# Rows and logits of an attention and mixture-of-experts kernel from one set of products on split rows, with expert weights laid out by the host

## The chip, the cores and the metric

The kernel runs on one core of one Trainium2 chip. The metric is the device time of one execution in microseconds, as the median of several runs; lower is better. The core has five engines that each work through an instruction stream of their own, in order: TensorE (PE, matrix products), VectorE (DVE), ScalarE (ACT), GpSimd (POOL) and SyncE (SP, which here issues almost all DMA transfers). Weight loads of PE are shown apart as PEld.

## The reference, cut to what matters

```python
def _attn_ref(u, v, z):                    # u, v: 8 x 2496 x 256, z: 8 x 2496 x 64
    scores = (1.0 / S) * np.matmul(z, z.transpose(0, 2, 1))
    attn = np.maximum(scores, 0.0) ** 2
    return u * np.matmul(attn, v)

def _moe_ref(x, modality_id, w_gate, modality_bias, w1, w2):   # x: 19968 x 256, 8 experts
    logits = x @ w_gate + modality_bias[modality_id]
    e_idx = np.argmax(logits, axis=1)
    gate_w = softmax(logits)[np.arange(N), e_idx]
    for e in range(E):
        mask = e_idx == e
        h = np.maximum(x[mask] @ w1[e], 0.0)                   # 256 -> 1024
        out[mask] = gate_w[mask, None] * (h @ w2[e])           # 1024 -> 256
```

The output of the attention, one row of 256 for each of 19968 tokens, is the input of the mixture of experts. Each token goes to the one expert with the largest logit.

## The kernel before, in words

**Precision.** Most products run in a rounded 32-bit type (`F32R`) that TensorE takes in one pass. To keep precision, an operand is split into a high part, its rounded copy, made by ACT or DVE, and a low part, the difference, made by DVE; then three products (high x high, high x low, low x high) replace one. What is handed to TensorE as plain 32-bit floats shows two recorded passes for each product.

**Attention stage.** There are 8 batches. The 2496 queries of a batch are cut into five chunks (`NCH`) of 512 columns, the last of 448. A chunk goes through ten steps (`NI`), each over 256 keys. A step forms the scores (`scores`, L307), takes ReLU and the square on ACT (`root`, `square`), splits the squares (`high`, `low`) and multiplies them with the split v (`weigh`, L418), adding up in PSUM. The 128 rows of the contraction are used as two halves of 64 that run side by side, so each accumulator exists twice; the two are added on the way out. Scores are symmetric: the squares of one block are turned by DVE in 32 x 32 blocks (`turn_squares`, L332), stored to HBM (`store_squares`, four to six DMA issues), and loaded later for the mirrored block (`load_turned`), which saves its scores.

**The end of a chunk.** The result lies with the 256 features on partitions (two groups of 128) and tokens along the free dimension, in the column order that the host has given to z and u. `evacuate_low` (ACT, L465) copies one accumulator half, `evacuate_high` (DVE, L469) adds the other, `weigh_u` (DVE, L476) multiplies with u. Then `make_gates` (PE, L492) forms the 8 logits of each token: for each of four tiles of 128 tokens and two groups of features a product in plain 32-bit floats on each half of the rows, 128 token columns stationary and the 8 gate columns moving. `take_gates` copies one half (ACT, L503) and adds the other (DVE, L505). `make_rows` (PE, L529) turns the same columns into rows by 16 transpositions against an identity matrix, and `take_rows` (ACT, L538, twice) puts them into the tile `x` of 128 tokens x 4 x 258, whose last two columns later take gate weight and token number. After a batch's last chunk the routing (`route_logits` to `route_slots`, mostly DVE, two small counting products on PE at L610) finds each token's expert and its place there, and GpSimd scatters the rows into the experts' lists `xs` in HBM by indirect DMA (`scatter`, L646), 20 for a batch.

**Expert weights.** `lay_weights` copies the weights from HBM to HBM into the layout that the expert stage loads: w1 of an expert in two copies (L206), its rows regrouped in blocks of 32, w2 in one copy (L211). These 24 copies are issued during batches two to seven, three to a batch's worth of steps.

**The order of the work.** The instruction order of every engine in the attention stage is written out by a planner when the program is built: each piece of work has an engine, a price in us, a due time in steps (`need`), predecessors with a lag, and buffers that it takes and gives back (`room`: 6 PSUM banks, 6 `zm` buffers, 7 `x` tiles and so on; 8 `lane`s stand for outstanding transfers of SP's queue). The planner keeps a clock for each engine and gives it the most urgent piece that is ready. On the chip every engine then follows that fixed order and waits by semaphore. The last chunk of the last batch is finished inside the expert stage (`between`).

**Expert stage.** From about 1390 us on: tiles of 512 tokens of one expert, up (L1224), ReLU and split (L1228, L1229), down (L1237, L1238), the weighted sum (L1272, L1275), and an indirect DMA that puts rows in place (L1247). The change touches only its first tile and the routing that lies in it.

Of the kernel before, what the change touches and what calls it, by code (L numbers as in the profile page):

```python
# [9 lines left out]
F32 = mybir.dt.float32  # L10
F32R = mybir.dt.float32r
# [4 lines left out]
P = 128  # L16
# [10 lines left out]
def tile_attention_moe(ctx: ExitStack, tc: tile.TileContext, ut, v, zt, mid, wg, mb, w1, w2, out):  # L27
# [15 lines left out]
    E, _, F = w1.shape  # L43
# [50 lines left out]
    def bank_tile(shape, name):  # L94
        return bank["pool"].tile(shape, F32, tag=bank["tag"], name=name)
# [73 lines left out]
    gate = small.tile([P, KD, E], F32, name="gate_w")  # L169
    small_raw = {}  # L170

    def load_gate():
        nc.sync.dma_start(out=gate, in_=wg.rearrange("(k p) e -> p k e", p=P))

# [27 lines left out]
    def lay_weights(e, n):  # L202
        if n == 0:

            for k in range(KD):
                nc.sync.dma_start(  # L206
                    out=w1s[e, :, k, :].rearrange("(b q) f -> b q f", q=BLK),
                    in_=w1[e].rearrange("(b k q) f -> k b q f", k=KD, q=BLK)[k],
                )
        else:  # L210
            nc.sync.dma_start(out=w2s[e], in_=w2[e].rearrange("(j p) d -> p j d", p=P))  # L211
# [47 lines left out]
    def load_u(b, c):  # L259
        x = rows.tile([P, KD, T], F32, tag="u", bufs=1, name="ut")  # L260
        nc.sync.dma_start(out=x, in_=ut[b, :, :, c * T:(c + 1) * T].rearrange("k p q -> p k q"))
        U[b, c] = x
# [192 lines left out]

    def evacuate_low(b, c, h):

        w = width[c]
        if not h:
            x = rows.tile([P, J, XW], F32, tag="x", bufs=NCH + 2, name="x")  # L460
            t = x.rearrange("p j c -> p (j c)")[:, 0:KD * T].rearrange("p (k t) -> p k t", k=KD)
            if w < T:
                nc.gpsimd.memset(t[:, :, w:T], 0.0)
            oT[b, c] = (t, x)
        nc.scalar.copy(out=oT[b, c][0][:, h, :w], in_=acc[b, c][1][h][:, :w])  # L465

    def evacuate_high(b, c, h):
        y = oT[b, c][0][:, h, :width[c]]
        nc.vector.tensor_tensor(out=y, in0=acc[b, c][0][h][:, :width[c]], in1=y, op=ALU.add)  # L469
        if not h:  # L470
            acc.pop((b, c))

    def weigh_u(b, c):

        t = oT[b, c][0]
        nc.vector.tensor_tensor(out=t, in0=t, in1=U.pop((b, c)), op=ALU.mult)  # L476

    turned_rows, gates = {}, {}

    def make_gates(b, c):  # L480

        t = oT[b, c][0]
        if b == B - 1 and c == NCH - 1:
            parts = [bank_tile([P, J, E], "pg")]
            rows_of = (slice(0, P),)
        else:
            parts = [bank_tile([P, J, E], "pg") for _ in halves]
            rows_of = halves
        for j in range(J):
            for dh in range(KD):  # L490
                for x, h in zip(parts, rows_of):
                    nc.tensor.matmul(  # L492
                        out=x[:, j, :], lhsT=key_columns(t[h, dh], c * J + j), rhs=gate[h, dh, :],
                        start=dh == 0, stop=dh == KD - 1,
                    )
        gates[b, c] = parts

    def take_gates(b, c, n):
        if c == 0 and n == 0:
            LG[b] = rows.tile([P, NCOL, E], F32, tag="lg", bufs=2, name="lg")  # L500
        y = LG[b][:, c * J:(c + 1) * J, :]
        if n == 0:
            nc.scalar.copy(out=y, in_=gates[b, c][0])  # L503
        else:
            nc.vector.tensor_tensor(out=y, in0=gates[b, c][1], in1=y, op=ALU.add)  # L505

    def make_last_rows(b, c):

        t, x = oT[b, c]
        parts = [bank_tile([P, J // 2, D], "po") for _ in range(2)]  # L510
        for j in range(J):
            for dh in range(KD):
                nc.tensor.transpose(  # L513
                    out=parts[j // 2][:, j % 2, dh * P:(dh + 1) * P], in_=key_columns(t[:, dh], c * J + j), identity=ident
                )
        turned_rows[b, c] = (parts, x)

    def take_last_rows(b, c, n):
        parts, x = turned_rows[b, c]
        nc.scalar.copy(out=x[:, n * J // 2:(n + 1) * J // 2, 0:D], in_=parts[n])  # L520
        X[b, c] = x

    def make_rows(b, c):
        t, x = oT[b, c]
        parts = [bank_tile([P, J, KD, DK], "po") for _ in halves]
        for j in range(J):
            for dh in range(KD):
                for r, h in enumerate(halves):
                    nc.tensor.transpose(  # L529
                        out=parts[r][:, j, dh, :], in_=key_columns(t[h, dh], c * J + j), identity=ident[h, h]  # L530
                    )
        turned_rows[b, c] = (parts, x)

    def take_rows(b, c, r):

        parts, x = turned_rows[b, c]
        y = x[:, :, 0:D].rearrange("p j (k h d) -> p j k h d", k=KD, h=2)[:, :, :, r, :]
        nc.scalar.copy(out=y, in_=parts[r])  # L538
        if r:
            del turned_rows[b, c]  # L540
            X[b, c] = x
# [351 lines left out]
    def transfer(us, need, f, *args, issues=1, take=(), **more):  # L893
        p = piece("Q", us, need, f, *args, take=[*take, *(Hold("lane") for _ in range(issues))], **more)
        p.issues = issues
        return p

    def piece(on, us, need, f, *args, after=(), take=(), drop=(), gate=-1):
# [6 lines left out]
        "zr": 3, "vr": 3, "x": NCH + 2, "u": 1, "lane": 8,  # L905
    }
    LEAD = 3.6
    MADE = 2
# [18 lines left out]
    def z_pieces(b, c):  # L927
        need = uses_z[b, c][0] - LEAD
        read = None
        if b:  # L930
            hold_zr[b, c] = Hold("zr")
            read = transfer(0.7, need - 4, load_z, b, c, take=[hold_zr[b, c]], gate=need - 25)
        high = piece("A", 0.55, need - 1, prep_z_high, b, c, after=[read], take=[hold_z[b, c]])
        done_z[b, c] = piece("D", 0.65, need - 0.6, prep_z_low, b, c, after=[high], drop=[hold_zr[b, c]])
        begun.append(done_z[b, c])
# [74 lines left out]
    def chunk_pieces(b, c):  # L1010
# [24 lines left out]
        taken[b, c] = [g1] + took  # L1035
        whole = c == NCH - 1 and b < B - 1
        if whole or b == B - 1 and c == 1:
            route_pieces(b, WHOLE if whole else SOON, end + 1.5, [p for k in range(c + 1) for p in taken[b, k]])
# [23 lines left out]
    transfer(0.3, 2, load_gate)  # L1062
# [7 lines left out]
    for e in range(E):  # L1070
        for k in range(2):
            n = 2 * e + k
            transfer(3.2, (1 + n // 3) * per + NI + NI // 2 * (n % 3), lay_weights, e, k, issues=1 if k else 2, gate=(1 + n // 3) * per + NI - 2 + NI // 2 * (n % 3))
# [25 lines left out]
    with tc.manual_schedule(engines={ET.PE, ET.Activation, ET.DVE, ET.Pool, ET.SP}):  # L1099
# [25 lines left out]
        releases, moved = [], 0.0  # L1125
# [26 lines left out]
        while left:  # L1152
# [24 lines left out]
            if e == "Q":  # L1177
                clock[e] = now + 0.4 * p.issues
                moved = max(clock[e] + 0.5, moved) + p.us
                p.end = moved + 1.1  # L1180
                releases += [(p.end, "lane")] * p.issues
# [19 lines left out]
        weigh_u(B - 1, NCH - 1)  # L1201
# [167 lines left out]
    between[0][1] += [lambda: make_last_rows(B - 1, NCH - 1)]  # L1369
    between[0][1] += [lambda: make_gates(B - 1, NCH - 1), lambda: take_gates(B - 1, NCH - 1, 0)]  # L1370
    between[0][2] += [lambda: take_last_rows(B - 1, NCH - 1, 0), lambda: take_last_rows(B - 1, NCH - 1, 1)]
# [8 lines left out]
    for slot, pieces in ((3, (route_logits, route_exp)), (4, (route_places,)), (5, (route_gates,)), (6, (route_count,)), (7, (route_slots,))):  # L1380
        put(slot, *(lambda p=p: p(B - 1, LATE) for p in pieces))
    for n, k in enumerate(range(LATE.start, NCOL)):
        put(8 + n * 5 // 6, lambda k=k: scatter(B - 1, k))
    planning = plan()
    for slot in (9, 10, 11, 12, 13):
        put(slot, lambda: next(planning, None))
# [84 lines left out]
```

## Time and profile before

| | |
|---|---|
| median of 3 runs | 2282.15 us (2278.42 to 2285.0) |
| profiled execution | 2283.72 us, span of its instructions 2281.9 us |
| mean granted clock of TensorE | 0.984 |
| busy: PE, DVE, ACT, POOL | 2235.4, 1555.8, 1338.1, 351.7 us |
| gate products, L492 | 1264 records, 85.2 us busy |
| transposes of rows, L529 | 624 records, 41.7 us busy |
| HBM read and written | 246.49 MB, 140.96 MB |

All figures below the first row come from one profiled execution. In rows of groups, "busy" is the time in which at least one instruction of the group ran and the mean is the duration of one; products overlap (weight load, two halves of the rows, pipeline), so a mean is not the time that a product takes from its successor. In a timeline row the first number is the start, the second how long the row's instructions lasted together, and `x32` how many of them are merged; a bracket gives the idle time before it and what ended it.

### The profile page before, as it was taken

The page shows a single profiled execution, that of the slowest core. Times are in us where ns is not written, and L with a number is a line of the kernel's source. Part 1 is how long each engine was busy: PE and PEld are TensorE (multiplying, and loading weights), DVE is VectorE, ACT ScalarE, POOL GpSimd, SP SyncE. Part 2 cuts the span into 40 slices and gives each one's busy share as a digit, 9 for nine tenths or more (in the row PEclk, how much of TensorE's full clock was granted, in tenths as well). Part 3 has the DMA queues.
Part 4 walks back from the last instruction along what each step waited for, and adds up shares of the span by engine and source line. Part 5 has one row for each costly group of instructions (what it writes and reads, how often), then busy time and mean ns, then how long its engine had stood idle before and what let it go on. Part 6 is the DMA issues. An engine that isn't in the chain of part 4 may idle for free. (4 is left out here: it accounts for less than half of the span.)

```text
span 2281.9 us, 43759 instructions
## 1 busy us (share of the span) xinstructions
PE 2235.4 (98%) x17166; PEld 1941.6 (85%) x17166; DVE 1555.8 (68%) x2163; ACT 1338.1 (59%) x1695; POOL 351.7 (15%) x342
## 2 busy tenths in 40 slices
PE   9999999999899999999999999999999999999997
PEld 8888988788799789799888888888888888888886
DVE  8667667677577767667877766666666666666664
ACT  8647658557457557557657663455555555554553
POOL 0000300300300300300300311211121212112121
PEclk9999999999999999999999999999999999999999
DMA  7975875884784884794884972554454545455450
GB/s 165 242 208 119 227 223 112 226 230 90 214 234 101 229 230 110 197 251 109 210 228 106 206 195 53 143 155 139 139 155 123 167 120 157 125 153 144 134 160 23
DMA packets 601378, 373.66 MB, mean 164 GB/s; under 512 B 487594, under 2 KB 550570, under 8 KB 596426
## 3 DMA queue, kind: packets, MB, share of 16 engines
q1 hardware_dynamic: 586074, 329.57, 56.6%
q0 software_dynamic: 15088, 41.21, 4.8%
q8 instruction: 136, 2.23, 0.4%
q14 instruction: 80, 0.66, 0.1%
HBM read 246.49 MB, written 140.96 MB: 170 GB/s over the span
## 5 line engine op out<-in xcount | busy, mean ns | idle before, releaser
L394 DVE TENSOR_TENSOR al<-r,ah 128x1024 fp32r<-128x1024 f32 (+1 forms) x359 | 422.3, 1191 | 85.4 <-ACT ah L385 77.0
L418 PE MATMUL acc<-ah,vh 64*128 64x512 f32 (+1 forms) x3120 | 465.9, 391 | 5.4 <-ACT x L465 3.1
L1237 PE MATMUL po<-w,hh 128*128 128x512 f32 x1248 | 449.9, 397 | 0.0
L418 PE MATMUL acc<-ah,vl 64*128 64x512 f32 (+1 forms) x3120 | 449.8, 385 | 0.0
L418 PE MATMUL acc<-al,vh 64*128 64x512 f32 (+1 forms) x3120 | 449.4, 384 | 0.0
L1224 PE MATMUL ph<-xh,w 128*128 128x512 f32 x1248 | 426.3, 392 | 0.5 <-ACT lg L503 0.3
L1228 ACT ACTIVATE hh<-ph 128x512 fp32r<-128x512 f32 x312 | 186.5, 598 | 381.7 <-PE ph L1224 381.5
L1229 DVE SCALAR_TENSOR_TENSOR hl<-ph,hh 128x512 fp32r<-128x512 f32 x312 | 215.8, 692 | 231.1 <-ACT hh L1228 231.1
L646 POOL DMA_INDIRECT xs<-x,sloti x160 | 193.9, 1212 | 1159.0 <-ACT r L315 516.2
L418 PEld LDWEIGHTS acc<-ah,vh 64*128 64x128 f32 x3120 | 327.8, 188 | 50.7 <-ACT x L465 6.0
L315 ACT ACTIVATE r<-s 128x1024 f32<-128x1024 f32 (+2 forms) x244 | 247.0, 1013 | 199.1 <-PE s L307 180.3
L418 PEld LDWEIGHTS acc<-al,vh 64*128 64x128 f32 x3120 | 328.5, 186 | 41.0 <-DVE al L397 0.8
L418 PEld LDWEIGHTS acc<-ah,vl 64*128 64x128 f32 x3120 | 323.9, 187 | 41.9
L1238 PE MATMUL po<-w,hl 128*128 128x256 f32 x1248 | 350.2, 281 | 0.0
L385 ACT CAST ah<-r 128x1024 fp32r<-128x1024 f32 (+1 forms) x257 | 261.5, 1029 | 96.6 <-PE acc L418 45.9
L1237 PEld LDWEIGHTS po<-w,hh 128*128 128x128 f32 x1248 | 234.5, 188 | 55.8
L1224 PEld LDWEIGHTS ph<-xh,w 128*128 128x128 f32 x1248 | 234.3, 188 | 54.9 <-DVE x L469 0.7
L1247 POOL DMA_INDIRECT out_dram<-y,ids x157 | 152.8, 973 | 761.5 <-DVE y L1275 733.1
L361 ACT ACTIVATE r<-r 128x1024 f32<-128x1024 f32 (+2 forms) x243 | 255.2, 1051 | 6.3
L332 DVE STREAM_TRANSPOSE turn<-r 128x1024 f32<-128x1024 f32 x158 | 196.0, 1241 | 91.1 <-DMA squares<-turn 61.8
L1224 PE MATMUL ph<-xl,w 128*128 128x512 f32 x624 | 245.0, 393 | 0.0
L1238 PEld LDWEIGHTS po<-w,hl 128*128 128x128 f32 x1248 | 235.0, 188 | 9.5
(157 smaller groups left out, 2015.7 us busy)
## 6 DMA issues: line engine op xcount, KB each, us to landing
squares<-turn SPq DMA_DIRECT2D x508, 128.0 KB
r<-squares SPq DMA_DIRECT2D x96, 512.0 KB
w<-w1s SPq DMA_DIRECT2D x37, 1024.0 KB
w<-w2s SPq DMA_DIRECT2D x37, 1024.0 KB
r<-squares SPq DMA_DIRECT2D x62, 448.0 KB
ut<-in_ut_dram SPq DMA_DIRECT2D x40, 512.0 KB
xg<-xs SPq DMA_DIRECT2D x156, 128.0 KB
vr<-in_v_dram SPq DMA_DIRECT2D x32, 512.0 KB
```

The costliest lines, as they stand in the source:

```text
L315: nc.scalar.activation(out=r[:, t, :w], in_=s[t][:, :w] if g < 2 else s[:, :, :w], func=AF.Relu, scale=INV)
L332: nc.vector.transpose(out=y.rearrange(order, n=2), in_=st_a[g].rearrange("p n (t i) -> p n t i", i=BLK))
L361: nc.scalar.square(out=a[:, t, :w], in_=r[:, t, :w])
L385: copy(out=ah[:, :, :w], in_=st_a[g][:, :, :w])
L394: nc.vector.tensor_tensor(out=al[:, :, :w], in0=a[:, :, :w], in1=ah[:, :, :w].bitcast(F32), op=ALU.subtract)
L418: nc.tensor.matmul(out=acc[b, c][r][dh][:, :w], lhsT=V[b, k // J][y][halves[r], k % J, dh * P:(dh + 1) * P], rhs=x[halves[r], k % 2, :w], ...
L646: nc.gpsimd.indirect_dma_start(out=xs, out_offset=bass.IndirectOffsetOnAxis(ap=RT[b]["sloti"][:n, k:k + 1], axis=0), in_=x[:n, j, :], in_o ...
L1224: nc.tensor.matmul(out=ph, lhsT=lhs, rhs=rhs[:, k, :], start=n == 0, stop=n == 3 * KD - 1)
L1228: nc.scalar.activation(out=hh, in_=ph, func=AF.Relu)
L1229: nc.vector.scalar_tensor_tensor(out=hl, in0=ph, scalar=0.0, in1=hh.bitcast(F32), op0=ALU.max, op1=ALU.subtract)
L1237: nc.tensor.matmul(out=po[j], lhsT=hh[:, s], rhs=both, start=f == 0, stop=False, skip_group_check=True)
L1238: nc.tensor.matmul(out=po[j][:, 0:D], lhsT=hl[:, s], rhs=w[:, 0, :], start=False, stop=f == KF - 1, skip_group_check=True)
```

## The change

- The result of a chunk is kept in tile order from the evacuation on: `by_tile` gives the evacuations an interleaved reading of the accumulator, so that the 128 columns of a tile lie side by side. The host hands in u in the same order. The last chunk of a batch is evacuated in three pieces for each group of features.
- After the multiplication with u the rows are split: `rows_high` (ACT) and `rows_low` (DVE), each into a buffer of the `zm` kind.
- One set of products gives rows and logits: stationary are 128 columns of the high or low part, moving are 80 columns, `mover` = [64 x 64 identity, 8 columns gate high, 8 columns gate low]. For a chunk these are 32 products in the rounded type, in two calls of `make_rows` for two tiles each. `take_rows` (ACT) copies the 64 identity columns to the rows and the 16 others to `sums`, four times a chunk; `take_gates` (DVE) adds the parts of a logit by a reduction over 256 columns.
- The gate is split once at the start (`prep_gate`).
- The host hands in w1 and w2 in the layout of the expert stage, and `lay_weights` copies them in eight parts of 32 rows for each expert, 64 copies in all, one each four steps from the second chunk of the second batch on.
- The planner: `lane`s are no longer held as buffers but modelled by a list of landing times; due times of `weigh_u`, the rows and the routing are later; z's high parts may not be made earlier than four steps ahead.
- In the expert stage the last chunk's rows come at the fourth and fifth group of the first tile, not the second, and the routing pieces behind them three places later.

```diff
     def lay_weights(e, n):
-        if n == 0:
-            for k in range(KD):
-                nc.sync.dma_start(
-                    out=w1s[e, :, k, :].rearrange("(b q) f -> b q f", q=BLK),
-                    in_=w1[e].rearrange("(b k q) f -> k b q f", k=KD, q=BLK)[k],
-                )
-        else:
-            nc.sync.dma_start(out=w2s[e], in_=w2[e].rearrange("(j p) d -> p j d", p=P))
+        dst, src = ((w1s, w1), (w2s, w2))[n // 4]
+        rows_of = slice(n % 4 * BLK, (n % 4 + 1) * BLK)
+        nc.sync.dma_start(out=dst[e, rows_of], in_=src[e, rows_of])
...
+    def by_tile(c, y, x, h):
+        x = x[:, :, h * P:(h + 1) * P]
+        if c < NCH - 1:
+            return [(y.rearrange("q (s p n) -> q s n p", s=2, n=2), x.rearrange("q (s n) p -> q s n p", s=2))]
...
+    def rows_high(b, c):
+        hi = turned.tile([P, J, D], F32R, tag="zm", bufs=NCH + 1, name="rh")
+        nc.scalar.copy(out=hi, in_=oT[b, c][:, :, 0:D])
+        parted[b, c] = [hi]
+
+    def rows_low(b, c):
+        hi = parted[b, c][0]
+        lo = turned.tile([P, J, D], F32R, tag="zm", bufs=NCH + 1, name="rl")
+        nc.vector.tensor_tensor(out=lo, in0=oT[b, c][:, :, 0:D], in1=hi.bitcast(F32), op=ALU.subtract)
+        parted[b, c].append(lo)
...
+    def make_rows(b, c, n):
+        parts = turned_rows[b, c] = [bank_tile([P, J // 2, KD, DK + GW], "po") for _ in halves]
+        for j in range(J // 2):
+            for dh in range(KD):
+                for m, x in enumerate(parted[b, c]):
+                    for y, h in zip(parts, halves):
+                        nc.tensor.matmul(
+                            out=y[:, j, dh, :], lhsT=x[h, n * J // 2 + j, dh * P:(dh + 1) * P], rhs=mover[h, dh, :],
+                            start=m == 0, stop=m == 1,
+                        )
...
+        nc.scalar.copy(out=x, in_=y[:, :, :, 0:DK])
+        nc.scalar.copy(out=sums[b, c][:, tiles, :, r, :], in_=y[:, :, :, DK:])
...
+        nc.vector.tensor_reduce(out=LG[b][:, c * J:(c + 1) * J, :], in_=y, axis=AX.X, op=ALU.add)
...
-        x = piece("D", 1.18, end + 0.1, weigh_u, b, c, after=[highs[1], read], drop=[hold_u[b, c]])
-        hold_r, hold_g = [Hold("bank"), Hold("bank")], [Hold("bank"), Hold("bank")]
-        g = piece("P", 1.1, end + 0.5, make_gates, b, c, after=[(x, 0.15)], take=hold_g)
-        g0 = piece("A", 0.2, end + 0.4, take_gates, b, c, 0, after=[(g, 0.25)], drop=hold_g[:1])
-        g1 = piece("D", 0.2, end + 0.4, take_gates, b, c, 1, after=[g0], drop=hold_g[1:])
-        r = piece("P", 0.6, end + 0.9, make_rows, b, c, after=[(x, 0.15), (g, 0.0), done_once.get("ident")], take=hold_r)
-        took = [piece("A", 0.52, end + 0.9 + 0.1 * k, take_rows, b, c, k, after=[(r, 0.25)], drop=hold_r[k:k + 1]) for k in range(2)]
+        x = piece("D", 1.18, end + 1.5, weigh_u, b, c, after=[highs[1], read], drop=[hold_u[b, c]])
+        own = [Hold("zm"), Hold("zm")]
+        h = piece("A", 0.95, end + 1.8, rows_high, b, c, after=[x], take=own[:1])
+        p = piece("D", 1.18, end + 2.2, rows_low, b, c, after=[(h, 0.12)], take=own[1:])
+        parts_of = own
+        took = []
+        for k in range(2):
+            own = [Hold("bank"), Hold("bank")]
+            p = piece("P", 0.46, end + 3 + 0.3 * k, make_rows, b, c, k, after=[(p, 0.15), done_once["gate"]], take=own, drop=parts_of if k else [])
+            took += [piece("A", 0.42, end + 3.2 + 0.3 * k, take_rows, b, c, k, r, after=[(p, 0.25)] + took[-1:], drop=own[r:r + 1]) for r in range(2)]
...
-            transfer(3.2, (1 + n // 3) * per + NI + NI // 2 * (n % 3), lay_weights, e, k, issues=1 if k else 2, gate=(1 + n // 3) * per + NI - 2 + NI // 2 * (n % 3))
+    for n in range(8 * E):
+        start = per + NI + n * 4
+        transfer(1.6, start + 4, lay_weights, n // 8, n % 8, gate=start)
```

More of the change, by code (lines that the diff above doesn't have):

```diff
@@ L166, in load_rows, with prep_gate @@
             nc.sync.dma_start(out=dst[64:P, J - 1:J, :], in_=tail)
-    gate = small.tile([P, KD, E], F32, name="gate_w")
+    GW = 2 * E
+    mover = small.tile([P, KD, DK + GW], F32R, name="mover")
     small_raw = {}
     def load_gate():
+        gate = raw.tile([P, KD, E], F32, tag="gate_w", name="gate_w")
         nc.sync.dma_start(out=gate, in_=wg.rearrange("(k p) e -> p k e", p=P))
+        small_raw["gate"] = gate
+    def prep_gate():
+        gate = small_raw.pop("gate")
+        high, low = mover[:, :, DK:DK + E], mover[:, :, DK + E:]
+        nc.vector.tensor_copy(out=high, in_=gate)
+        nc.vector.tensor_tensor(out=low, in0=gate, in1=high.bitcast(F32), op=ALU.subtract)
+        for h in halves:
+            for k in range(KD):
+                nc.vector.tensor_copy(out=mover[h, k, 0:DK], in_=eye[h, h])
     brow = small.tile([P, 2, E], F32, name="brow")
@@ L259, in load_u @@
     def load_u(b, c):
-        x = rows.tile([P, KD, T], F32, tag="u", bufs=1, name="ut")
-        nc.sync.dma_start(out=x, in_=ut[b, :, :, c * T:(c + 1) * T].rearrange("k p q -> p k q"))
+        x = rows.tile([P, J, D], F32, tag="u", bufs=1, name="ut")
+        nc.sync.dma_start(out=x, in_=ut[b, :, c * J * D:(c + 1) * J * D].rearrange("p (j d) -> p j d", j=J))
         U[b, c] = x
@@ L454, in tile_attention_moe @@
     oT, X, LG = {}, {}, {}
+    def by_tile(c, y, x, h):
+        x = x[:, :, h * P:(h + 1) * P]
+        if c < NCH - 1:
+            return [(y.rearrange("q (s p n) -> q s n p", s=2, n=2), x.rearrange("q (s n) p -> q s n p", s=2))]
+        return [
+            (y[:, 0:H].rearrange("q (p n) -> q n p", n=2), x[:, 0:2]),
+            (y[:, H:H + P], x[:, 2]),
+            (y[:, H + P:LAST], x[:, 3, 0:LAST - H - P]),
+        ]
     def evacuate_low(b, c, h):
-        w = width[c]
         if not h:
[L460 to L465, printed above, removed]
+            x = oT[b, c] = rows.tile([P, J, XW], F32, tag="x", bufs=NCH + 2, name="x")
+            if c == NCH - 1:
+                nc.gpsimd.memset(x[:, J - 1, 0:D].rearrange("q (k p) -> q k p", k=KD)[:, :, 64:P], 0.0)
+        for y, x in by_tile(c, acc[b, c][1][h], oT[b, c], h):
+            nc.scalar.copy(out=x, in_=y)
     def evacuate_high(b, c, h):
-        y = oT[b, c][0][:, h, :width[c]]
-        nc.vector.tensor_tensor(out=y, in0=acc[b, c][0][h][:, :width[c]], in1=y, op=ALU.add)
+        for y, x in by_tile(c, acc[b, c][0][h], oT[b, c], h):
+            nc.vector.tensor_tensor(out=x, in0=y, in1=x, op=ALU.add)
         if not h:
@@ L473, in weigh_u @@
     def weigh_u(b, c):
[L475 to L489, printed above, removed]
-            for dh in range(KD):
[L491 to L496, printed above, removed]
@@ L498, in take_gates @@
-    def take_gates(b, c, n):
-        if c == 0 and n == 0:
-            LG[b] = rows.tile([P, NCOL, E], F32, tag="lg", bufs=2, name="lg")
[L501 to L541, printed above, removed]
+        x = oT[b, c][:, :, 0:D]
+        nc.vector.tensor_tensor(out=x, in0=x, in1=U.pop((b, c)), op=ALU.mult)
+    def rows_high(b, c):
+        hi = turned.tile([P, J, D], F32R, tag="zm", bufs=NCH + 1, name="rh")
+        nc.scalar.copy(out=hi, in_=oT[b, c][:, :, 0:D])
+        parted[b, c] = [hi]
@@ L893, in transfer @@
     def transfer(us, need, f, *args, issues=1, take=(), **more):
-        p = piece("Q", us, need, f, *args, take=[*take, *(Hold("lane") for _ in range(issues))], **more)
+        p = piece("Q", us, need, f, *args, take=take, **more)
         p.issues = issues
@@ L932, in z_pieces @@
             read = transfer(0.7, need - 4, load_z, b, c, take=[hold_zr[b, c]], gate=need - 25)
-        high = piece("A", 0.55, need - 1, prep_z_high, b, c, after=[read], take=[hold_z[b, c]])
+        high = piece("A", 0.55, need - 1, prep_z_high, b, c, after=[read], take=[hold_z[b, c]], gate=int(need - 4))
         done_z[b, c] = piece("D", 0.65, need - 0.6, prep_z_low, b, c, after=[high], drop=[hold_zr[b, c]])
@@ L1061, in tile_attention_moe @@
     done_once["ident"] = piece("D", 2.2, 6, prep_constants)
-    transfer(0.3, 2, load_gate)
+    p = transfer(0.3, 2, load_gate)
+    done_once["gate"] = piece("D", 0.9, 7, prep_gate, after=[p])
     p = transfer(2.0, 8, load_modality, issues=7, gate=6)
@@ L1177, in tile_attention_moe @@
             if e == "Q":
[L1178 to L1181, printed above, removed]
+                for _ in range(p.issues):
+                    now = max(now, landed[-LANES]) + 0.4
+                    moved = max(now + 0.5, moved) + p.us / p.issues
+                    landed.append(moved + 1.1)
+                clock[e], p.end = now, landed[-1]
             for h in p.take:
@@ L1200, in tile_attention_moe @@
             evacuate_high(B - 1, NCH - 1, h)
-        weigh_u(B - 1, NCH - 1)
+        for f in (weigh_u, rows_high, rows_low):
+            f(B - 1, NCH - 1)
     ph1.close()
@@ L1459 @@
     inputs["zt"] = _np.tile(inputs["z"].transpose(0, 2, 1)[:, :, cols], (1, 2, 1))
-    inputs["ut"] = inputs["u"].transpose(0, 2, 1).reshape(b, 2, d // 2, s)[:, :, :, cols]
+    order = _np.concatenate([
+        _np.arange(whole).reshape(-1, 128, 4).transpose(0, 2, 1).ravel(), tail, _np.tile(_np.arange(s - 64, s), 2)
+    ])
+    inputs["ut"] = inputs["u"][:, order].reshape(b, -1, 128, 2, 128).transpose(0, 4, 1, 3, 2).reshape(b, 128, -1)
+    w1, w2 = inputs["moe_w1"], inputs["moe_w2"]
+    e, _, f = w1.shape
+    inputs["moe_w1"] = w1.reshape(e, 4, 2, 32, f).transpose(0, 1, 3, 2, 4).reshape(e, 128, 2, f)
+    inputs["moe_w2"] = w2.reshape(e, -1, 128, d).transpose(0, 2, 1, 3)
     arrays, args = {}, []
```

37 lines of the change are left out of this document (23 added, 14 removed).

## The prediction, made before the changed kernel had run

> **What bounds the kernel now.** I read the page first, then what TensorE (PE) waited for, then the timeline at a chunk's end, and then the DMA queue ahead of the longest wait.
>
> ```profile
> span 2281.9 us, 43759 instructions
> PE 2235.4 (98%) x17166; PEld 1941.6 (85%) x17166; DVE 1555.8 (68%) x2163; ACT 1338.1 (59%) x1695; POOL 351.7 (15%) x342
> ```
> PE is busy in 98% of the span, so a microsecond taken out of PE's queue is a microsecond of the kernel, unless a wait takes its place. ACT and DVE have about a third of the span to spare. The remaining idle time of PE has one main cause (columns: total us, times, longest):
>
> ```profile
> PE pg L492 <- DVE x L476: 19.1, 4, 9.7
> PE s L307 <- ACT r L315: 3.8, 4, 1.4
> PE acc L418 <- ACT x L465: 3.1, 3, 1.5
> PE acc L418 <- ACT ah L385: 2.3, 2, 2.0
> ```
> Four times the gate products stood at the head of PE's queue for DVE's multiplication with u (L476), 19.1 us together. All else is small. So there are two things to price: what the gate products and transposes take of PE while it runs, and these four waits.
>
> **PE's share of a chunk's end, before.** A chunk is turned at its end by 16 gate products (two passes each, 32 records) and 16 transposes. They come in pairs, one on each half of the rows, so I follow one half. In a chunk without a wait:
>
> ```profile
> 539.29 0.17 PE L492 MATMUL pg<-gate_w,x 64*128 64x8 f32 x1
> 539.32 1.89 PE L492 MATMUL pg<-gate_w,x 64*128 64x8 f32 x29
> 541.03 0.47 PE L418 MATMUL acc<-ah,vh 64*128 64x512 f32 x1
> ...
> 543.89 0.21 PE L529 MATMUL po<-ident,x 64*128 64x64 f32 x1
> 544.56 0.50 PE L307 MATMUL s<-zm 64*128 64x512 f32 x1
> ```
> From the first gate product to the next useful product on that half: 541.03 - 539.29 = 1.74 us for 16 passes. For the transposes: 544.56 - 543.89 = 0.67 us for 8. Together 2.41 us a chunk. The first of a burst costs only 0.03 us (539.29 to 539.32), the others (1.74 - 0.03) / 15 = 0.114 us each, though only 8 columns move: the loading of the 128 stationary columns sets the pitch.
>
> **The same after.** A chunk then has two bursts (make_rows for n = 0 and 1), each of 16 products, so 8 on each half, in the rounded type and with 80 moving columns. The nearest rows in type are the two counting products of the routing, also rounded, with 8 columns:
>
> ```profile
> 551.53 0.25 PE L610 MATMUL pc<-cnt,ones 64*128 64x8 f32 x1
> 551.64 0.48 PE L307 MATMUL s<-zm 64*128 64x512 f32 x1
> ...
> 551.78 0.25 PE L610 MATMUL pc<-cnt,ones 64*128 64x8 f32 x1
> 551.89 0.71 PE L307 MATMUL s<-zm 64*128 64x512 f32 x4
> ```
> The last small product holds its half for 0.11 us on both halves. So a burst is 0.03 + 7 x 0.11 = 0.80 us and a chunk 1.60 us. Saved: 0.81 us a chunk. The 39 chunks are those of these groups (1248 = 39 x 32 records, 624 = 39 x 16):
>
> ```profile
> L492 PE MATMUL pg<-gate_w,x 64*128 64x8 f32 x1248 | 83.3, 263 | 19.1 <-DVE x L476 19.1
> L529 PE MATMUL po<-ident,x 64*128 64x64 f32 x624 | 41.7, 267 | 0.8 <-ACT lg L503 0.8
> ...
> L1103 PE MATMUL warm<-zeros 64*128 64x512 f32 x12 | 2.9, 643 | 0.0
> ...
> L1103 PE MATMUL warm<-zeros 64*128 64x128 f32 x8 | 1.1, 427 | 1.0 <-POOL zeros L101 1.0
> ```
> 39 x 0.81 = 31.6 us. Bounds: at the transposes' pitch ((0.67 - 0.03) / 7 = 0.091 us) a chunk takes 1.34 us and 42 us go. The other side is whether 80 columns of the rounded type stay under the load. The only narrow rounded products in the trace are the warm-up's: four pairs of 128 columns took 1.1 us (0.28 a pair) beside six of 512 in 2.9 us (0.48 a pair), at the slower clock of the start. They aren't charged like full ones, but a pitch of half again cannot be excluded: at 0.14 us a chunk takes 2.02 us and only 15 us go. I take 0.11, the row of the same type on the same halves.
>
> **The four waits.** The longest, with the DMA queue ahead of it:
>
> ```profile
> 601.67 1.40 SPq L206 DMA_DIRECT2D w1s<-in_moe_w_dram  x2
> 603.18 11.32 SPq L344 DMA_DIRECT2D squares<-turn  x4
> 614.59 2.85 SPq L324 DMA_DIRECT2D r<-squares  x1
> ...
> 619.31 1.25 DVE L332 STREAM_TRANSPOSE turn<-r 128x1024 f32<-128x1024 f32 x1 [9.88 <-DMA squares<-turn]
> ...
> 621.78 3.58 PE L492 MATMUL pg<-gate_w,x 64*128 64x8 f32 x32 [9.66 <-DVE x L476]
> ...
> 604.00:608.00 4.00, 4.00 (x38) 3.84 (x36) 4.00 (x8) 3.64 (x6) 2.01 (x2) 1.00 0.71 242
> 612.00:616.00 4.00, 0.12 (x2) 0.00 (x0) 0.00 (x0) 0.00 (x0) 0.00 (x0) 1.00 0.58 153
> 616.00:620.00 4.00, 0.00 (x0) 0.00 (x0) 0.69 (x1) 0.00 (x0) 0.00 (x0) 0.59 0.60 159
> 624.00:628.00 4.00, 4.00 (x28) 3.44 (x28) 2.68 (x5) 1.27 (x3) 1.83 (x2) 0.50 0.92 353
> ```
> (The last four are stretches: length, busy time and count of PE, PEld, DVE, ACT and POOL, granted clock, DMA share, GB/s.) Right behind two w1 copies SP needs 11.32 us to issue four stores of turned squares; DVE's next transposition waits 9.88 us for a buffer of those stores, the multiplication with u stands behind it on DVE, and PE behind that. All the while the DMA engines are only 0.58 to 0.60 busy: the w1 copies don't fill them, they hold places in the queue. A wait costs more than its length: the clock is 0.59 to 0.50 afterwards, the gate products take 3.58 us in place of some 1.9, and the four microseconds from 624 hold 28 products in place of 38 (1.05 us lost). That is 2.7 us each; the four cost 19.1 + 11 = 30 us.
>
> The change lays each expert's weights in eight copies of 32 rows, source and target alike, one each four steps, in place of three larger ones. It also moves make_rows behind its inputs (due at end + 3, where make_gates was at end + 0.5), so that a late DVE has some three steps of other products as cover. I count 24 of the 30 us as gone, an estimate: all of the longest wait and of another like it, and half of two that came while the DMA engines were full with other transfers too (rows below). Were the cover gone, all 30 stay. On the w1 copies the Trainium skill has a rule: in "DMA: Bandwidth & Descriptors", the section on why a DMA increments its semaphore by 16, a DMA runs on the largest number up to 16 of engines that divides the slowest dimensions of both sides. The old w1 pattern begins with 4 blocks, so 4 engines; the new begins with 32 rows, so 16. The low DMA share above agrees; no run here shows it by itself.
>
> **What is added beside PE.** Rows for the prices:
>
> ```profile
> L237 ACT CAST vh<-vr 128x1024 fp32r<-128x1024 f32 x39 | 40.7, 1043 | 20.1 <-PE acc L418 19.3 <-DMA vr<-in_v_dram 0.7
> L256 DVE TENSOR_TENSOR vl<-vr,vh 128x1024 fp32r<-128x1024 f32 x39 | 47.6, 1221 | 17.3 <-ACT vh L237 17.1
> L538 ACT COPY x<-po 128x512 f32<-128x512 f32 x78 | 42.0, 591 | 53.4 <-PE po L529 50.6 <-DVE ah L385 1.5 <-DVE al L394 1.3
> L503 ACT COPY lg<-pg 128x32 f32<-128x32 f32 x40 | 7.4, 186 | 65.5 <-PE pg L492 65.4
> L505 DVE TENSOR_TENSOR lg<-pg,lg 128x32 f32<-128x32 f32 x39 | 7.3, 188 | 19.4 <-ACT lg L503 19.3
> L622 DVE TENSOR_REDUCE slot<-run 128x20 f32<-128x160 f32 x9 | 4.0, 445 | 0.3
> ```
> ACT: rows_high 1.04 us; take_rows is four times a copy of 256 and one of 64 columns. Between 186 ns for 32 and 591 ns for 512 that is 0.38 + 0.21, four times 2.36. Gone: 0.19 + 2 x 0.59. So 2.0 us more a chunk, 80 us in all. DVE: rows_low 1.22, the sum of the four parts of a logit 0.5 (445 ns for 160 columns, here 256), gone 0.19: 1.5 us more, 60 us in all. Both lie beside PE's steps and make no term themselves; what they can do is lengthen PE's small waits on ACT, 3.8 + 3.1 + 2.3 = 9.2 us now. I add 5 us (from 0 to 25). The interleaved reading of the accumulators in tile order moves the same columns and I price it at nothing; the last chunk of a batch does it in three pieces, two more fixed starts of under 0.19 us for each half on each of ACT and DVE, beside the next batch's products. The ut load keeps its size, and prep_gate is six small DVE copies once. rows_high and rows_low take two of the six zm buffers that the next batch's z needs; the plan holds them for some two steps.
>
> **The entry to the expert stage.** There the last chunk has nothing behind it:
>
> ```profile
> 1390.70 0.60 ACT L1228 ACTIVATE hh<-ph 128x512 fp32r<-128x512 f32 x1 [1.02 <-PE ph L1224]
> 1390.96 1.23 DVE L476 TENSOR_TENSOR x<-x,ut 128x1024 f32<-128x1024 f32 x1
> 1392.43 1.07 PE L513 MATMUL po<-ident,x 128*128 128x128 f32 x8
> 1393.34 1.90 PE L492 MATMUL pg<-gate_w,x 128*128 128x8 f32 x16
> ```
> rows_high waits for L476 (until 1392.2) and stands on ACT ahead of the first hh; rows_low then ahead of the first hl. The first down products come some 2 us later than PE could take them, while the 3 us of transposes and gates become 1.6 us. I put +2 us (from -1 to +5).
>
> **Sum**, against the profiled execution's 2283.7 us (its span of 2281.9 and 1.8 around it; 1.6 above the median of 2282.15): 2283.7 - 31.6 - 24 + 5 + 2 = 2235 us. On the median that is 2233.5; I say 2234.
>
> **Rivals.** *The waits stay.* The queue is as full with 64 small copies as with 24 large ones, and a late store still stops DVE. Beside this, the Trainium skill ("DMA: Bandwidth & Descriptors", the section on the anatomy of one DMA) gives each DMA a fixed cost of about 2 us, by a fit for another issue path. For: in two of the four waits the DMA engines were full (DMA share next to last):
>
> ```profile
> 440.00:444.00 4.00, 1.06 (x10) 1.06 (x12) 4.00 (x5) 1.45 (x2) 1.69 (x1) 0.83 1.04 283
> 790.00:794.00 4.00, 1.96 (x17) 1.30 (x13) 2.23 (x3) 0.64 (x1) 0.65 (x1) 1.00 1.06 276
> ```
> Then 2283.7 - 31.6 + 5 + 2 = 2259 us. *Given back.* The narrow products cost 0.14 us (15 us saved), the four waits stay, and ACT's waits take 10 us: 2283.7 - 15 + 10 + 2, about 2281, no change that a measurement can tell (0.3% of 2282, 7 us, is about what it can). *PE waits for the longer chain.* Between L476 and the rows now stand an ACT cast and a DVE subtraction, 1.04 + 1.22 = 2.26 us, and PE's order is fixed by a plan whose ACT price (0.42 us for what I make 0.59) is too low. If PE stands for that chain in all 39 chunks, +88 us: 2283.7 - 31.6 + 88 = 2340 us. It decides from 0.8 us a chunk. Against it: now PE waits at this place in 4 chunks of 39, in the longest behind a late DMA, and the new due time lies steps later.
>
> **How the numbers follow.** Forecast 2234: 0.68. Waits stay, 2259: 0.17. Given back, 2281: 0.05. Chain, 2340: 0.10. The low end takes the transposes' pitch (10 us more), all four waits (6) and no ACT waits (5): 2234 - 21, with a little for the DMA waits inside ACT and DVE, 2208. The high end reaches past 2259 with 10 us more of ACT waits, 2270; "given back" and "chain" are left out. Faster by over 0.3%: 0.85; within: 0.05; slower: 0.10.
>
> **What would show it.** Right: make_rows at about 0.8 us of PE for each burst; no PE wait over 3 us at it; the waits of DVE on squares and of SP on its queue shrunk; ACT some 80 us and DVE some 60 us busier. Wrong: a pitch near 0.14 us or more; PE idle at make_rows behind rows_low in many chunks; z or accumulator waits at the batches' borders; or stores of squares still held for 10 us.

## The result, and the profile after

| | before | after |
|---|---|---|
| median | 2283.57 us (2278.42 to 2286.71, 4 runs) | 2190.53 us (2189.61 to 2191.02, 4 runs) |
| ratio | | 0.9594, 95% interval 0.9575 to 0.9613 |
| profiled execution, its span | 2283.72, 2281.9 us | 2189.61, 2187.7 us |
| first up product of the expert stage at | 1389.0 us | 1293.5 us |
| from there to the end | 892.9 us | 894.2 us |

The kernel is 93 us faster. I had said 2234 us with 2208 to 2270: the sign was right, the gain was nearly twice what I forecast, and the time lies below the range. All of it is in the attention stage, which is 95.5 us shorter; the expert stage is 1.3 us longer.

The page of the kernel after, first the totals (busy us, share, instructions), then the slices of PE and of its granted clock:

```profile
span 2187.7 us, 42980 instructions
PE 2168.1 (99%) x16550; PEld 1879.4 (86%) x16550; DVE 1612.7 (74%) x2231; ACT 1404.0 (64%) x1978; POOL 360.3 (16%) x342
...
PE   9999999999999999999999999999999999999997
...
PEclk9999999999999999999999999999999999999999
```

What PE waited for in the kernel after, all of it (total us, times, longest):

```profile
PE po L1237 <- issue: 2.3, 1, 2.3
PE s L314 <- ACT zm L230: 1.9, 1, 1.9
PE warm L1101 <- POOL zeros L101: 1.0, 1, 1.0
PE s L314 <- DVE zm L235: 0.6, 1, 0.6
PE ph L1224 <- DVE x L485: 0.6, 1, 0.6
PE ph L1224 <- DVE xl L866: 0.3, 1, 0.3
```
The 19.1 us at the gate products are gone, and so is every other wait inside the attention stage: what is left lies in its first 12 us and at the entry to the expert stage. The attention stage as one stretch from 16 us on, first of the kernel before, then of the kernel after (length, busy us and count of PE, PEld, DVE, ACT, POOL, granted clock, DMA share, GB/s):

```profile
16.00:1389.00 1373.00, 1343.93 (x12676) 1190.34 (x12672) 967.82 (x1329) 890.48 (x1018) 184.26 (x155) 0.98 0.72 183
```

```profile
16.00:1293.00 1277.00, 1276.81 (x12038) 1128.42 (x12036) 1023.27 (x1392) 954.72 (x1290) 192.92 (x155) 1.00 0.77 197
```
PE's idle time went from 1373.00 - 1343.93 = 29.1 us to 0.2 us, and the clock from 0.98 to 1.00. PE's busy time fell by 67 us with all weighted sums and scores kept, twice the 31.6 us forecast for the products that went, so a busy PE had not been a PE at its pace. I split the stage in three for every kernel below, by stretches of 4 us from its start to the first up product: *idle* is length minus PE's busy time, *clock* is PE's busy time times (1 - granted clock), the rest is products at full pace. Before: 32.7 idle, 24.2 clock, 1332.1 products. After: 3.7, 1.3, 1288.5. So the 95.5 us are 29.0 of idle time, 22.9 of clock and 43.6 of products.

The products of a chunk's end in the kernel after, in the timeline:

```profile
413.28 0.20 PE L514 MATMUL po<-mover,rh 64*128 64x80 f32 x2
413.32 0.28 PE L514 MATMUL po<-mover,rl 64*128 64x80 f32 x2
413.42 0.28 PE L514 MATMUL po<-mover,rh 64*128 64x80 f32 x2
...
413.98 0.29 PE L514 MATMUL po<-mover,rl 64*128 64x80 f32 x2
414.09 1.17 PE L425 MATMUL acc<-ah,vh 64*128 64x512 f32 x8
415.10 1.07 PE L425 MATMUL acc<-ah,vl 64*128 64x512 f32 x8
```
A burst takes 414.09 - 413.28 = 0.81 us, against 0.80 forecast, at 0.11 us a pair: 80 columns cost no more than 8 did.

### The profile page after: what moved, and what is told of

The parts are those of the page before. It is cut to its first block, busy times and chain, and to the rows that moved or that the text cites. A ratio compares the mean times of both kernels' runs of the same rounds, so it can differ in the third digit from the quotient of the medians.

```text
span 2187.7 us, 42980 instructions
## 1 busy us (share of the span) xinstructions
PE 2168.1 (99%) x16550; PEld 1879.4 (86%) x16550; DVE 1612.7 (74%) x2231; ACT 1404.0 (64%) x1978; POOL 360.3 (16%) x342
## 5 line engine op out<-in xcount | busy, mean ns | idle before, releaser
L425 PE MATMUL acc<-ah,vh 64*128 64x512 f32 (+1 forms) x3120 | 451.2, 386 | 0.1
L1237 PE MATMUL po<-w,hh 128*128 128x512 f32 x1248 | 448.2, 396 | 2.3 <-issue 2.3
L425 PE MATMUL acc<-al,vh 64*128 64x512 f32 (+1 forms) x3120 | 439.4, 382 | 0.0
L425 PE MATMUL acc<-ah,vl 64*128 64x512 f32 (+1 forms) x3120 | 438.5, 383 | 0.0
L640 POOL DMA_INDIRECT xs<-x,sloti x160 | 202.5, 1266 | 1064.9 <-ACT ah L392 772.0
L425 PEld LDWEIGHTS acc<-al,vh 64*128 64x128 f32 x3120 | 319.6, 185 | 40.8
L425 PEld LDWEIGHTS acc<-ah,vh 64*128 64x128 f32 x3120 | 317.1, 185 | 43.5 <-ACT x L481 0.7
L425 PEld LDWEIGHTS acc<-ah,vl 64*128 64x128 f32 x3120 | 313.6, 185 | 41.9
L392 ACT CAST ah<-r 128x1024 fp32r<-128x1024 f32 (+1 forms) x268 | 272.5, 1031 | 32.0 <-PE acc L425 26.4
L1237 PEld LDWEIGHTS po<-w,hh 128*128 128x128 f32 x1248 | 234.7, 188 | 57.1 <-issue 2.7
```

What stands on the lines that cost most here:

```text
L392: copy(out=ah[:, :, :w], in_=st_a[g][:, :, :w])
L425: nc.tensor.matmul(out=acc[b, c][r][dh][:, :w], lhsT=V[b, k // J][y][halves[r], k % J, dh * P:(dh + 1) * P], rhs=x[halves[r], k % 2, :w], ...
L640: nc.gpsimd.indirect_dma_start(out=xs, out_offset=bass.IndirectOffsetOnAxis(ap=RT[b]["sloti"][:n, k:k + 1], axis=0), in_=x[:n, j, :], in_o ...
L1237: nc.tensor.matmul(out=po[j], lhsT=hh[:, s], rhs=both, start=f == 0, stop=False, skip_group_check=True)
```

## The experiments

Names that begin with b change the kernel before, with a the changed kernel. The theory after the result, *copies*: the old copies of the weights made the waits, and the waits made the slow clock; what the products save comes on top. Its rival, *plan*: the new order of the work (later due times, another model of SP's transfers) removed them. Medians are given with the ratio to the kernel before in the same session; the last two columns are the split just described.

| | median us | ratio, 95% interval | idle | clock |
|---|---|---|---|---|
| before | 2281.2 to 2287.3 | | 32.7 | 24.2 |
| after | 2190.5 | 0.9594 [0.9575, 0.9613] | 3.7 | 1.3 |
| b_copies | 2238.2 | 0.9800 [0.9782, 0.9818] | 9.3 | 5.1 |
| a_oldcopies | 2227.5 | 0.9752 [0.9733, 0.9770] | 27.8 | 14.5 |
| b_lanes | 2292.4 | 1.0037 [1.0023, 1.0052] | 43.7 | 20.8 |
| a_oldlanes | 2200.6 | 0.9638 [0.9620, 0.9656] | 9.3 | 1.4 |
| b_three | 2237.7 | 0.9799 [0.9783, 0.9815] | 9.1 | 5.4 |
| b_small4 | 2237.7 | 0.9795 [0.9779, 0.9811] | 8.6 | 8.4 |
| b_small16 | 2237.0 | 0.9794 [0.9778, 0.9810] | 9.2 | 5.2 |
| a_twice | 2262.3 | 0.9903 [0.9887, 0.9920] | 3.6 | 1.4 |
| b_w1 | 2235.6 | 0.9800 [0.9778, 0.9823] | 10.6 | 3.8 |
| b_w2 | 2276.8 | 0.9980 [0.9965, 0.9995] | 30.9 | 24.0 |
| b_three_turns | 2271.9 | 0.9955 [0.9937, 0.9972] | 9.7 | 5.2 |
| a_early | 2191.9 | 0.9604 [0.9583, 0.9625] | 4.0 | 3.0 |
| b_order | 2240.6 | 0.9795 [0.9780, 0.9810] | 9.0 | 5.5 |
| a_order | 2192.8 | 0.9588 [0.9573, 0.9603] | 3.7 | 1.3 |
| a_entry | 2190.1 | 0.9573 [0.9560, 0.9586] | 4.0 | 1.3 |

**The copies, or the plan?** Four kernels, one part moved in each.

b_copies, the new copies and the host's layout of the weights in the kernel before:

```diff
-            transfer(3.2, (1 + n // 3) * per + ..., lay_weights, e, k, issues=1 if k else 2, gate=...)
+    for n in range(8 * E):
+        start = per + NI + n * 4
+        transfer(1.6, start + 4, lay_weights, n // 8, n % 8, gate=start)
```

> The kernel before with one part of the change: the host lays out w1 and w2, and 64 copies of 32 rows take the place of 24. Theory 'copies' (the waits of TensorE and the slower clock behind them, 29 us idle and 23 us of clock in the attention stage, come from the old weight copies): about 2284 - 52 = 2232 us, TensorE idle in the attention stage under 8 us. Theory 'plan' (the new model of SP's outstanding transfers and the later due times removed them): 2284 us, idle near 30 us.

a_oldcopies, the reverse in the changed kernel:

> The changed kernel with the old weights: no layout by the host, 24 copies with their old times. Theory 'copies': the waits come back, 2190 + 52 = about 2242 us. Theory 'plan': 2190 us, since the due times and the model of the transfers are kept and cover a late transfer.

b_lanes and a_oldlanes, the model of SP's outstanding transfers alone, put in and taken out:

```diff
-                clock[e] = now + 0.4 * p.issues
-                moved = max(clock[e] + 0.5, moved) + p.us
+                for _ in range(p.issues):
+                    now = max(now, landed[-LANES]) + 0.4
+                    moved = max(now + 0.5, moved) + p.us / p.issues
+                    landed.append(moved + 1.1)
```

> The kernel before with the planner's new model of SP's outstanding transfers alone (a list of landing times in place of eight held lanes). Theory 'copies': 2284 us within 7. Theory 'plan', by this model: some 30 us or more faster, to 2254 us or less, with fewer and shorter waits of DVE for stores of squares.

> The changed kernel with the old model of SP's outstanding transfers (eight held lanes). Theory 'copies': 2190 us within 7. Theory 'plan', by this model: 2215 us or more, with waits at the rows or the squares.

The copies alone gave 45 us: idle time fell from 32.7 to 9.3 us and the clock's share from 24.2 to 5.1, 42.5 us of the 45. Taken out of the changed kernel they cost 37 us, idle 3.7 to 27.8 and clock 1.3 to 14.5. *Copies* holds, a little short of its 52 us, since the 9.3 us idle and 5.1 us of clock of b_copies lie ahead of the first weight copy (210.7 us in the kernel before): at the stage's start, and in waits on ACT between 148 and 192 us. *Plan* falls as the main cause. Its model of the transfers alone made the kernel before 9 us slower, while the changed kernel is 10 us slower without it. With the old copies in place the waits behind them only move. What PE waited for, first in a_oldcopies, then in b_lanes:

```profile
PE po L520 <- ACT rh L502: 15.2, 3, 6.6
PE po L520 <- DVE rl L508: 4.7, 5, 1.2
```

```profile
PE po L529 <- ACT lg L503: 23.9, 4, 8.6
PE pg L492 <- DVE x L476: 11.5, 5, 8.5
```
Whatever stands first at the end of a chunk pays for the late transfer. The later due times did not cover it.

*Plan* has a smaller part all the same, the waits on ACT between 148 and 192 us. That stretch in before, b_copies, b_lanes and a_oldlanes, one line each in this order:

```profile
148.00:192.00 44.00, 38.99 (x335) 34.17 (x334) 26.05 (x29) 27.71 (x32) 0.00 (x0) 0.84 0.53 132
148.00:192.00 44.00, 38.33 (x345) 34.89 (x343) 26.36 (x29) 27.59 (x32) 0.00 (x0) 0.88 0.50 122
148.00:192.00 44.00, 44.00 (x461) 41.95 (x459) 32.70 (x40) 30.46 (x36) 0.00 (x0) 1.00 0.39 98
148.00:192.00 44.00, 39.61 (x377) 34.39 (x375) 34.99 (x42) 36.78 (x53) 0.00 (x0) 1.00 0.55 132
```
PE idles 5.0 us there before and 5.7 us with the new copies; the model of the transfers alone leaves 0.0, and without it the changed kernel idles 4.4 us again. So that model removes these waits, although behind the w1 copies (from 192 us on) it makes the idle time of the kernel before grow from 24.1 to 40.2 us. How it does so is open.

**Which property of the copies?** The new copies differ in four ways: host's layout, size, number and times. b_three keeps the old number, sizes and times and takes the host's layout; b_small4 and b_small16 do without the host and cut the copies small.

```diff
 b_three
+                nc.sync.dma_start(out=w1s[e, k * 64:(k + 1) * 64], in_=w1[e, k * 64:(k + 1) * 64])
 b_small4: w1 in eight copies of 4 x 8 rows; b_small16: in eight of one block of 32 rows
+                out=w1s[e, :, k, :].rearrange("(b q) f -> b q f", q=BLK)[:, r],
+                out=w1s[e, b * BLK:(b + 1) * BLK, k, :], in_=w1[e].rearrange("(b k q) f -> k b q f", k=KD, q=BLK)[k, b]
```

> The kernel before with the host's layout of the weights, but still 24 copies at the old times and of the old sizes (w1 in two of 64 rows of 8 KB, w2 in one). Theory 'shape' (the old copies are slow because of their pattern: w1 in four blocks, w2 in rows of 1 KB): nearly all of the 45 us that 64 copies gave, 2245 us or less. Theory 'burst' (1 MB at once fills SP's queue, whatever its pattern): over 2265 us, waits at the gate products as before.

> The kernel before, weights not laid out by the host, but cut small and spread: w1 of an expert in eight copies of 128 KB that keep the pattern of four blocks (4 x 8 rows), w2 in four parts, 96 copies in all over the same steps as the 64. Theory 'shape': the w1 copies stay slow, so at most half of the 45 us, 2260 us or more. Theory 'burst': 2240 us within 7.

> As the one with 4 x 8 rows, same sizes, count and times, but each w1 copy takes one block of 32 rows. Theory 'shape': 2240 us, clearly below the one with four blocks. Theory 'burst': the same as the one with four blocks within 7 us.

All three give the whole 46 us. So neither theory was right alone: the 24 large copies do no harm in another layout, and the slow pattern does none in small pieces that are spread out. (The clock share of b_small4, 8.4 us against 5.2, is not left over from it: all of it lies before 192 us, and its first w1 copy is issued at 226.7 us.) That there are 96, 64 or 24 copies makes no difference either: 2237.0 and 2237.7, 2238.2, 2237.7 us. The Trainium skill's fixed cost of some 2 us for each DMA ("DMA: Bandwidth & Descriptors", the anatomy of one DMA, which prices another issue path) does not show in these times.

b_w1 and b_w2 give the host's layout to w1 alone and to w2 alone, with the old numbers and times:

> The kernel before with the host's layout for w1 alone, two copies of 64 rows an expert at the old times; w2 as before. Theory 'w1' (the pattern of four blocks is what held SP's queue): 2238 us within 7. Theory 'w2' (1 MB in pieces of 1 KB held it): 2275 us or more. If each did its share: in between.

> The kernel before with the host's layout for w2 alone, one copy an expert at the old time, each partition's 8 KB in one piece; w1 as before. Theory 'w1': 2284 us within 7, the waits at the gate products behind w1 copies still there. Theory 'w2': 2245 us or less. If each did its share: in between.

It is w1: 46 us by w1, 4 us by w2. In b_w2 PE's wait stands where it stood:

```profile
PE pg L492 <- DVE x L476: 16.0, 4, 9.6
```
The last pair changes the order of two dimensions in the w1 copies and nothing else: same bytes, same pieces of 4 KB, same sizes, number and times, no host.

```diff
-                    out=w1s[e, :, k, :].rearrange("(b q) f -> b q f", q=BLK),
-                    in_=w1[e].rearrange("(b k q) f -> k b q f", k=KD, q=BLK)[k],
+                    out=w1s[e, :, k, :].rearrange("(b q) f -> q b f", q=BLK),
+                    in_=w1[e].rearrange("(b k q) f -> k q b f", k=KD, q=BLK)[k],
```

> The kernel before with the two outer dimensions of the w1 copies written in the other order (32 rows outside, four blocks inside), nothing else: the same bytes in the same pieces of 4 KB, the same sizes, count and times, no layout by the host. Theory 'engines' (a copy runs on as many DMA engines as its outer dimension allows, 4 before): 2238 us within 7. Theory 'pieces' (the 8 KB pieces of the host's layout made the copies fast): 2284 us within 7.

> The changed kernel without the host's layout and with the 24 old copies, w1 with 32 rows outside and four blocks inside. Theory 'engines': 2190 us within 7, so the host's layout and the 64 copies are not needed. Theory 'pieces': 2227 us, as with the old copies.

Both as *engines* says: 46.8 us in the kernel before, and 2192.8 us for the changed kernel with the old 24 copies, against 2190.5 with the new 64 (the intervals overlap). SP's queue and the DMA share at the same place of the program in b_order (the prediction shows it for the kernel before):

```profile
581.01 1.39 SPq L206 DMA_DIRECT2D w1s<-in_moe_w_dram  x2
582.49 3.50 SPq L344 DMA_DIRECT2D squares<-turn  x4
586.09 2.91 SPq L324 DMA_DIRECT2D r<-squares  x1
...
584.00:588.00 4.00, 4.00 (x40) 3.65 (x38) 2.06 (x5) 3.75 (x5) 1.11 (x2) 1.00 1.03 388
588.00:592.00 4.00, 4.00 (x38) 3.67 (x36) 3.85 (x7) 2.91 (x4) 1.17 (x2) 1.00 1.12 309
```
The four stores behind the two copies are issued in 3.50 us, not 11.32, and the DMA engines are full: 1.03 and 1.12, where the kernel before had 0.71 at about the same distance behind the copies (604 to 608 us) and 0.58 and 0.60 after that. From 192 us to the first up product PE idles 0.1 us in b_order, against 24.1 us before, and the clock stays full. This is what the rule of the Trainium skill gives that the prediction cites: four entries in the outer dimension, four engines; 32, sixteen.

No view here counts engines by copy, but the packed trace, from which the views are made, has start, length and size of every packet. The pair of w1 copies ahead of this one is followed by one load of squares, 384 packets of 4 KB in all. In the kernel before they have landed 15.9 us after SP began to issue the pair (564.89 us), in b_order 7.5 us after (549.61 us). From 573 to 580 us in the kernel before exactly four of them are under way at once for 5.2 of the 7 us, and never more than six; from 551 to 557 us in b_order it is 14 or more for 4.2 of the 6 us. Four at a time agrees with four engines; which engine a packet took the trace does not say. That the order of the dimensions decides is measured.

**The price of the narrow products.** a_twice does each product of make_rows twice; b_three_turns does each transposition twice, on top of b_three.

```diff
-                for m, x in enumerate(parted[b, c]):
+                for m, x in enumerate(parted[b, c] * 2):
...
-                for r, h in enumerate(halves):
+                for r, h in 2 * list(enumerate(halves)):
```

> The changed kernel with each product of make_rows done twice (the second pair overwrites the first with the same values): 16 pairs more a chunk. If a narrow product costs the 0.11 us that its successor waits (my term), 40 x 16 x 0.11 = 71 us more, 2261 us. If the 1.85 us a chunk that PE loses hold fixed parts (two starts, the break between the halves) and the product itself costs less, clearly under 2255 us; if the longer burst makes others wait, over 2270 us.

> The kernel before with the host's layout and 24 copies (2238 us), and each transposition of rows done twice into the same place: 8 pairs more a chunk, 39 chunks. At the pitch that I read on one half of the rows (0.091 us) 28 us more, 2266 us. If a transposition costs PE what the sum over clean stretches leaves for it beside 1.74 us of gate products (2.82 - 1.74 = 1.08 us for 8, 0.13 us), 41 us more, 2279 us.

a_twice is 71.7 us slower: 71.7 / (40 x 16) = 0.112 us a pair, the term as forecast. The transpositions cost 2271.9 - 2237.7 = 34.2 us, or 34.2 / (39 x 8) = 0.110 us a pair, not the 0.091 that I had read. With the rows of 8 columns in the prediction (0.114 us for each pass of a plain product, 0.11 for a rounded one), a pair costs about 0.11 us whether it moves 8, 64 or 80 columns, as product or as transposition; a chunk's end costs PE about the number of its pairs (each pass counted) times 0.11 us.

**The due times, and the entry.** a_early puts the due times of a chunk's end back to about the old ones; a_entry moves rows_high and rows_low of the last chunk behind the second group of the first expert tile.

```diff
-        p = piece("D", 1.18, end + 2.2, rows_low, ...)
+        p = piece("D", 1.18, end + 0.4, rows_low, ...)
...
-        for f in (weigh_u, rows_high, rows_low):
-            f(B - 1, NCH - 1)
+        weigh_u(B - 1, NCH - 1)
+    between[0][1] += [lambda: rows_high(*end), lambda: rows_low(*end)]
```

> The changed kernel with the due times of the chunk's end put back to about the old ones (weigh_u end + 0.1, rows_high + 0.3, rows_low + 0.4, make_rows + 0.5 and 0.6, take_rows + 0.9). Theory 'copies': nothing is late any more, 2190 us within 7. Theory 'cover' (the later due times are what keeps PE from waiting at the rows): PE waits at make_rows behind rows_low in many chunks, 2200 us or more.

> The changed kernel with the last chunk's rows_high and rows_low moved from the end of the attention stage behind the second group of the first expert tile, so that they no longer stand ahead of the first hh on ACT and the first hl on DVE. If the 2.3 us that PE waits at the first down product come from there: that wait is gone, about 2 us less, 2188 us, at the edge of what can be measured. If it comes from elsewhere: the wait stays.

a_early is the same as the changed kernel within what can be measured: with the transfers in time the longer chain to the rows needs no cover. (Its clock share of 3.0 us, against 1.3, is one longer slow spell in the first 20 us.) In a_entry the wait of 2.3 us at L1237 is gone from the list of PE's waits, so it came from where I had put it, but the median, 2190.1, cannot be told from 2190.5. None of the versions tried beats the changed kernel by a measurable amount.

## Why the prediction was wrong, point by point

- **What bounds the kernel.** Right: PE's queue did, and both what was taken out of it and the waits in it came back as time.
- **PE's share of a chunk's end.** The burst after was right (0.81 us, 0.80 forecast), the saving too small: 31.6 us forecast, and between b_order and after, with idle and clock taken out (1342.2 - 9.0 - 5.5 = 1327.7 against 1288.5), 39.2 us measured. The mis-sized part is the transpositions before, 0.67 us read off one half of the rows in one burst, whose pitch is 0.110 and not 0.091 us. Eight pairs fewer at 0.110 are 39 x 8 x 0.110 = 34.3 us; the other 5 us stay open.
- **The four waits: the step that failed**, "the four cost 19.1 + 11 = 30 us" and "I count 24 of the 30 us as gone". The mechanism was right: stores stood in SP's queue behind w1 copies that left the DMA engines half empty; and so was the rule beside it. The size was off by half: 29.0 us of idle time and 22.9 us of clock went, 51.9 in all. First, the copies cost more than I priced and all of it went, also the two waits that came while the DMA engines were full, which I had halved. From 192 us on the kernel before has 24.1 us idle and loses 15.8 us to the clock; b_order has 0.1 and 0.0. So 39.8 us went where I counted 24: I had added up only the idle time of the gate products, not the waits on ACT and on the transposes beside them, and priced the slow clock by the gate products and one stretch of 4 us. Second, I took the small waits on ACT for lasting and growing by 5 us. Between 148 and 192 us they cost 5.0 us idle and 5.5 us of clock, and all of that went. b_lanes, where all of it is gone too, and a_oldlanes, where 4.4 us of the idle time are back, put it down to the planner's new model of the transfers, for which the sum has no term. The remaining 1.6 us are a shorter slow spell in the first 20 us, and that is luck: such a spell costs 1.2 us in b_copies and 2.9 in b_small4, which are alike up to there.
- **Added work on ACT and DVE.** Right in size (ACT 66 us more, 80 forecast; DVE 57, 60 forecast) and on it lying beside PE. The 5 us of added waits did not come.
- **The entry.** 2 us forecast, 1.3 measured, and by the wait named.
- **The rivals.** None came. "The waits stay" because the queue is as full with 64 copies is refuted by b_copies, and b_small16 shows that 96 do no harm. "Chain" is refuted by the list of waits after, which has none at the rows. The plan's late due times, which I counted as a cover, are worth nothing (a_early).

The sum with the measured terms: 2283.7 - 39.2 - 29.0 - 22.9 + 1.3 = 2193.9, and 2189.6 was measured; the difference is 4.4 us of products (1332.1 to 1327.7) that went already between before and b_order, and these stay open.

## What to carry to other kernels

When an in-order engine stands still behind transfers while the DMA engines are only half busy, look for a copy whose outer dimension is small: here swapping two dimensions in one access pattern, 4 x 32 to 32 x 4, was worth 47 us, as much as all the rest of the change. Cutting the same copies small and spreading them did as much. Price a wait of TensorE with the slow clock that follows it, and add up idle time and lost clock over the whole stage, not only at the longest entry of the list of waits. Price products with few moving columns by their number, not by what they move: here 0.11 us for each pair, with 8, 64 or 80 columns.

## What the runs showed of the hardware that was not expected

The clock can drop after shorter pauses than I thought, and stays down for longer. Two spells of the kernel before, in stretches of one microsecond (granted clock third from last):

```profile
154.00:155.00 1.00, 1.00 (x15) 0.96 (x16) 0.92 (x2) 0.00 (x0) 0.00 (x0) 1.00 1.02 348
155.00:156.00 1.00, 0.35 (x5) 0.21 (x3) 0.46 (x1) 0.61 (x2) 0.00 (x0) 0.94 1.01 345
156.00:157.00 1.00, 0.00 (x0) 0.00 (x0) 0.00 (x0) 1.00 (x2) 0.00 (x0) 0.50 1.00 327
...
162.00:163.00 1.00, 1.00 (x10) 0.92 (x8) 0.50 (x1) 0.00 (x0) 0.00 (x0) 0.64 0.72 91
...
791.00:792.00 1.00, 0.96 (x9) 0.46 (x5) 0.23 (x1) 0.00 (x0) 0.00 (x0) 1.00 0.92 334
792.00:793.00 1.00, 0.00 (x0) 0.00 (x0) 1.00 (x3) 0.00 (x0) 0.00 (x0) 1.00 1.22 292
793.00:794.00 1.00, 0.00 (x0) 0.00 (x0) 1.00 (x3) 0.64 (x1) 0.65 (x1) 1.00 1.13 239
794.00:795.00 1.00, 0.75 (x8) 0.75 (x8) 1.00 (x2) 0.41 (x1) 1.00 (x1) 0.59 0.93 234
...
800.00:801.00 1.00, 1.00 (x8) 0.81 (x6) 0.08 (x1) 1.00 (x3) 0.67 (x1) 0.50 1.17 305
801.00:802.00 1.00, 1.00 (x12) 0.84 (x10) 0.73 (x2) 0.84 (x1) 0.30 (x1) 1.00 1.14 244
```
By these rows PE stops at 155.35 us and the clock halves at 155.9, right behind 3.6 us of gate products and transpositions; at 794.2 us it halves 2.2 us after PE stopped. Both spells last 6.8 us. The packed trace records each change of the granted clock: the eight half-clock spells in the attention stage of the kernel before last 3.41 us (one), 6.83 us (five), 10.24 us (one) and 13.65 us (one), all multiples of 3.41 us. The length of a pause alone does not decide: in the longest wait PE stopped at 612.1 us and the clock held until 616.7. The Trainium skill ("TensorE: Matmul & The Clock Gate", the part on oscillation in real kernels) warns of pauses over some 3.4 us; here 2.2 us and less were enough in two spells, while 4.6 us passed in a third, and the measurement decides. That the narrow products before the pause count as little activity would explain the first spell; no run here tests it.
